# Order of ACT's casts and of the DMA issues of P in a step of hashed attention with a feed-forward network

## The chip, the cores and the metric

One core of a Trainium2 chip. The kernel is one program on that core; its time is the device time in microseconds of one execution. Three runs of the kernel before were timed, and one more execution was profiled. Engines in the text: PE (TensorE, matrix products, with its weight loads PEld), DVE (VectorE), ACT (ScalarE), POOL (GpSimd), SP (SyncE, which issues nearly all DMAs).

## The reference

Attention in which a query sees only the keys that fall in the same hash bucket (six signs of a random projection), and a feed-forward network on the result. q, k and v are 4 x 8 x 768 x 64 (batches, heads, rows, width), the network is 512 to 2048 to 512, all in float32.

```python
q_bits = (np.einsum('bhsd,dk->bhsk', q, proj) > 0)      # k_bits likewise
mask = q_bucket[:, :, :, None] == k_bucket[:, :, None, :]
scores = np.where(mask, scale * np.matmul(q, k.transpose(0, 1, 3, 2)), -1e9)
attn = np.exp(scores - scores.max(-1, keepdims=True))
attn = attn / (attn.sum(-1, keepdims=True) + 1e-9)
x = np.matmul(attn, v).transpose(0, 2, 1, 3).reshape(B * S, H * D)
h = x @ w_in
out = (h * np.clip(h + 3.0, 0.0, 6.0) / 6.0) @ w_out
```

## The kernel before

The attention work is cut into 192 units g: 32 heads (batch by batch), each with six tiles of 128 queries against all 768 keys. The network's work is cut into chunks of 256 tokens, each with 16 slices of the hidden width. Every float32 operand of a product is split into a high part (a cast to the fp32r type) and a low part (the difference), and products are made of high and low parts.

The program has an opening with attention alone, a stretch with network work for batch 0, and from unit GT = 102 on the function `beside_ffn(k)`, one call for each step k, in which a unit of attention and a slice of the network advance together. When the attention is done, the rest of the network runs alone. The order of the instructions on PE, DVE, ACT and POOL is that of the program text; SP's order is set by a planner, which keeps dependences and the orders given by `issue_after(x)`: what is issued inside stands behind x in its queue.

In `beside_ffn(k)` for k of 102 and more a unit g goes through these stages:
- step g - 3, `lead`: the scores on PE (`scores`, L387 and L389).
- step g - 2, `lowest` (the row minimum on DVE, L396), `exponential` (ACT, L408), and `flip` (L426): DVE transposes P in 32 x 32 blocks (L429), and a DMA writes it to a DRAM tile `fd`, one of four.
- step g - 1, `move` (L434): four DMAs, the homes, read `fd` into one of two home tiles (`spare` for even g, `px` for odd g), each 32 rows; this finishes the transpose. A home is free again when unit g - 2 has been split.
- step g + 1, `split_p` (L451) for the two halves c of the keys: ACT casts the high part `ph` (L475); the low part `pl` is made by POOL for c = 1 (L477) and by DVE for c = 0 (L479; it is put in the list `lows`, and `split_lows()` issues it).
- odd step 2u + 3, `values_whole(u)`: the product of v with the units 2u and 2u + 1 together (PE, L513), and in `output` its copy and its DMA.

The network's work of a step is a generator `fill`; `go("A")` to `go("D")` let it advance if its next stage has that letter. A: the gate's cast `gb` (ACT, L689) and its low part (DVE, L690). B: the first product (`gemm1`, L661). C: the second product of the slice before (`gemm2`, L699, L700, L704) and the gate (ACT L683, DVE L684). D: small steps from the list `side` that prepare the next chunk: loads of x, the spread of 1/sum, a transposition of it on PE (`normalise`), the product with x (the list `muls`, issued by `multiply()`, DVE L590), and the splitting of x. `add()` issues the waiting accumulating DMAs from POOL; an entry put in `fresh` waits one call of `add()` longer than one in `adds`.

So in the old order a step of this stretch holds, on ACT: the gate's cast, the exponential of k + 2, the cast of half 1 of unit k - 1, the copy of the output, the gate's first function, the cast of half 0. On DVE: the minimum, the gate's low part, a normalising product if there is one, the transpose, the gate's product, the low part of half 0. In the steps with k % 6 = 2 the minimum comes behind the gate's stage A (`behind`). In SP's queue the write of unit k + 2 stands ahead of the homes of unit k + 1.

Of the kernel before, what the change touches and what calls it, by code (L numbers as in the profile page):

```python
# [28 lines left out]
LA = 3  # L29
# [3 lines left out]
LT = 1  # L33
# [10 lines left out]
def lsh_attention_moe(  # L44
# [10 lines left out]
    nc = tc.nc  # L55
# [3 lines left out]
    KT = S // P  # L59
# [14 lines left out]
    last = None  # L74

    def dma(out: bass.AP, in_: bass.AP):
        nonlocal last
        last = nc.sync.dma_start(out=out, in_=in_)  # L78

    paced = False  # L80
# [147 lines left out]
    NS = NJ * KT  # L228
# [3 lines left out]
    GT = GF + FT  # L232
# [139 lines left out]
    scs, probs, outs = {}, {}, {}  # L372
# [18 lines left out]
    def lowest(g: int):  # L391

        s = scs.pop(g)
        m = sp.tile([P, 1], F32, name=f"m{g}", tag="m", bufs=4)
        pr_ = sp.tile([P, 2, HW], F32, name=f"p{g}", tag="p", bufs=2)
        nc.vector.tensor_scalar(  # L396
            out=pr_[:], in0=s[:, :, :HW], scalar1=CAP, scalar2=None,
            op0=ALU.min, op1=ALU.min, accum_out=m[:],
        )
        probs[g] = pr_, m  # L400
# [20 lines left out]

    written, moved, homes = {}, {}, []

    def flip(g: int):  # L426
        nonlocal written
        x = probs.pop(g)[0][:].rearrange("p c k -> p (c k)")
        nc.vector.transpose(x, x)  # L429
        d = dp.tile([P, S], F32, name=f"fd{g}", tag="fd", bufs=4)  # L430
        dma(out=d[:], in_=x)
        written[g] = d, last

    def move(g: int):  # L434
        if not homes:
            px = sp.tile([P, S], F32, name="px", tag="ga", bufs=1)
            homes.extend([spare[0][:, :S], px[:]])
        to = moved[g] = homes[g % 2]
        d, _ = written.pop(g)
        after = written[g + 1][1] if g + 1 in written else last  # L440
        with tc.issue_after(after.ins):
            for x in range(4):
                r = slice(32 * x, 32 * x + 32)
                dma(
                    out=to[r].rearrange("b (i c) -> b i c", i=4),
                    in_=d[:].rearrange("(i b) (g c) -> g b i c", i=4, g=4)[x],
                )

    lent = []

# [32 lines left out]
    def split_lows():  # L483
        for f in lows:
            f()
        lows.clear()
# [31 lines left out]
    adds, fresh = [], []  # L518
# [10 lines left out]
    def output(un: int):  # L529
        nonlocal vdone  # L530
        i, u = divmod(un, KT // 2)
        b, h = divmod(i, H)
        o = (h % 2) * D
        acc = accs.pop(un)

        if u != 1:
            outs[i] = sp.tile([P, 4 * P if u == 0 else 2 * P], F32, name=f"y{i}_{u}", tag=f"y{u}", bufs=1)
        y = outs[i][:, 2 * P :] if u == 1 else outs[i][:, : 2 * P]

        r = slice(o, o + D)  # L540
        r2 = slice(D - o, 2 * D - o)
        last_head = h == H - 1 and u == (0 if b else 2)
        if last_head:
            nc.scalar.copy(y[r], acc[r2])
            nc.vector.tensor_add(y[r], acc[r], y[r])
        else:
            nc.scalar.copy(y, acc[:])
        if u or last_head:
            single = last_head or h == H - 1 and b
            c = slice(2 * u * P, 2 * (u + 1) * P) if single else slice(0, 4 * P) if u == 1 else slice(4 * P, S)  # L550
            to = xs[b][h * D : (h + 1) * D, c]

            with tc.issue_after(copied.ins):
                dma(out=to, in_=y[r] if single else outs[i][r])
            if not last_head:
                ts = (u,) if single or u else (0, 1)
                (fresh if single and u == 2 else adds).append((i, ts if u != 1 or single else (0, 1), to, y[r2] if single else outs[i][r2]))
        vdone = 2 * un + 2


# [36 lines left out]
    def multiply():  # L597
        for f in muls:
            f()
        muls.clear()  # L600
# [78 lines left out]
    def gate(n: str, fc: int, hg, copy, engine, between=lambda: None):  # L679

        hp, g = hg[:, 0], hg[:, 1]
        r = sp.tile([P, TC], F32, name=f"g{n}_{fc}", tag="g", bufs=1)
        nc.scalar.activation(r[:], hp, AF.Relu, bias=three[:], scale=1.0)  # L683
        nc.vector.scalar_tensor_tensor(out=g, in0=r[:], scalar=6.0, in1=hp, op0=ALU.min, op1=ALU.mult)  # L684
        between()

        def split():
            gh, gl = gate_tiles(f"{n}_{fc}")
            copy(gh, g)  # L689
            engine.tensor_sub(gl, g, gh.bitcast(F32))  # L690
            return gh, gl

        return split
# [31 lines left out]


    xr0, x0 = {}, {}
    side, opening, amid = [], [], []

    def beside():  # L730
        if side:
# [195 lines left out]
    def ffn():  # L927
# [5 lines left out]
        def there(c: int) -> bool:  # L933

            b, t = chunks[c]
            return vdone >= (b + 1) * HK - KT + 2 * (t + 1) and not pending(b, range(H), t)
# [40 lines left out]
        for c, (b, t) in enumerate(chunks):  # L977
            while not there(c):
                if pend is not None:
                    finish()()  # L980
                stage = "B"
                yield
            n = f"{b}_{t}"
            if c not in xr:
                begin(c)
            while side:
                beside()
                stage = "B"
                yield
                if not paced:  # L990
                    yield
            if c not in xhl:
                place(c)
                for cc in range(NCC):
                    split(c, cc)
            ffn_on = True
            copy = nc.scalar.copy
            po = None
            for fc in range(NFC):
                hp = gemm1(n, fc, xhl[c])  # L1000
                stage = "C"
                yield
                end = finish() if pend is not None else lambda: None
                if po is None:
                    po = ps.tile([P, 2, 512], F32, name=f"po{n}", tag="s" if b == B - 1 and t % 2 == 0 else "po", bufs=1)
                parted = paced
                split_g = gate(n, fc, hp, copy, nc.vector, lambda: amid and amid.pop()())
                if not parted:
                    gg = split_g()
                end()  # L1010
                if c + 1 < len(chunks) and c + 1 not in xr and there(c + 1):
                    if fc >= XF[chunks[c + 1][0] == B - 1]:
                        begin(c + 1)
                if parted:
                    stage = "D"
                    yield
                    for _ in range(-(-len(side) // (NFC - fc))):
                        beside()
                if fc + 1 == NFC and c + 1 in xr and c + 1 not in xhl and not side:
                    place(c + 1)  # L1020
                    for cc in range(NCC):
                        split(c + 1, cc)
                elif not parted:
                    beside()
                if parted:
                    stage = "A"
                    yield
                    gg = split_g()
                pend = ((b, t), (fc, [po[:, u] for u in range(2)], *gg))
                stage = "B"  # L1030
                yield
                if not parted:
                    beside()
            del xhl[c]
# [64 lines left out]
    with tc.manual_schedule(engines={ET.PE, ET.DVE, ET.Activation, ET.Pool}):  # L1099
# [9 lines left out]
        def go(part: str):  # L1109
            if stage == part:  # L1110
                next(fill, None)
# [3 lines left out]
        def beside_ffn(k: int):  # L1115
# [9 lines left out]
            for _ in range(2):  # L1125
                u = vnext // 2
# [6 lines left out]
                        through.append(vnext // 2 - 1)  # L1133
                if k < GT:
                    break
            behind = (k - 1 + LA) % KT == 4
            if GT <= k < NS - 2 and not behind:
                lowest(k + 2)
            go("A")
            if GT <= k < NS - 2 and behind:  # L1140
                lowest(k + 2)
            if k < GT:
                for c in range(2):
                    split_p(k, c, False)
# [13 lines left out]
            paced = True  # L1158
            multiply()
            if k + 2 < NS:  # L1160
                flip(k + 2)
            split = GT <= k - LT < NS
            if split:
                split_p(k - LT, 1, False)
            go("B")
            if k == NS + LT:
                homes.clear()
# [2 lines left out]
            hashed = k + LA < NS and (k + LA) % KT == 4 and (k + LA) // KT + 1 < NJ  # L1170
            if hashed:
                hash_qk((k + LA) // KT + 1)
            if split:
                amid.append(lambda: (split_p(k - LT, 0, False), split_lows()))
            go("C")
            while amid:
                amid.pop()()
            split_lows()
            if hashed:
                bits((k + LA) // KT + 1)  # L1180
            if k + LA < NS:
                lead(k + LA)
            if moves:
                moves.pop(0)()
            if GT <= k + 1 < NS:
                move(k + 1)

            place_in_chunk = (k - GT) % NFC
# [6 lines left out]
        for k in range(NS + LT + 2):  # L1195
# [4 lines left out]
            i, t = divmod(k, KT)  # L1200
# [74 lines left out]
        paced = False  # L1275
# [52 lines left out]
```

## Time and profile before

| | |
|---|---|
| median of three runs | 975.12 us (974.37, 975.12, 977.23) |
| the profiled execution | 973.11 us, span 971.3 us |
| granted clock of TensorE | 0.998 |
| PE busy in the span | 948.0 us, 98% |
| DVE, ACT, POOL busy | 723.5, 625.0, 473.6 us |
| first and last `fd` write | 397.1 and 800.8 us, 90 of them |

How to read the rows: a timeline row has the start in us, the duration in us, the engine, the line, the operation, output<-input and a count; in brackets the idle time of the engine ahead of it and what ended it. SPq is SP's queue: the duration is that of the issue, not of the transfer. A row of waits has who waited, for what, the total in us, how often, and the longest. A row of a window has its bounds and length, then for each of PE, PEld, DVE, ACT and POOL the busy time in us with the instructions, then the granted clock, the busy share of the 16 DMA engines and GB/s. A row that starts with a line number and ends with two times has minimum, median and maximum duration in ns, and the first and the last start. A row of DMA issues ends, where the profile knows it, with the median us from issue to landing.

### The profile page before, as it was taken

What the parts mean: (1) busy time and instruction counts of PE and PEld (TensorE: products, weight loads), DVE (VectorE), ACT (ScalarE), POOL (GpSimd) and SP (SyncE); (2) the same over time, 40 slices, a digit from 0 to 9 for tenths busy, and PEclk for the clock granted to TensorE, in tenths of its full rate; (3) what the DMA queues carried; (4) which work ended last, traced back from release to release, by engine and by line L of the source; (5) the groups of instructions that cost most, each with busy time, mean ns of one, the idle gap of its engine ahead of it and who ended that gap; (6) DMA issues with size and microseconds to landing.
All of it is one profiled execution on the core that took longest, in us unless ns stands there. A gap on an engine that the chain in (4) does not pass through costs nothing.

```text
span 971.3 us, 19460 instructions
## 1 busy us (share of the span) xinstructions
PE 948.0 (98%) x6306; PEld 873.6 (90%) x6306; DVE 723.5 (74%) x1470; ACT 625.0 (64%) x1421; POOL 473.6 (49%) x582
## 2 busy tenths in 40 slices
PE   8999999999999999899999999999999999999997
PEld 7999888999989999799899899989899899889896
DVE  7999988888569999877878878878777874342422
ACT  6898875655478988667766666666666664333332
POOL 6777744665537776455555545555545432000000
PEclk9999999999999999999999999999999999999999
DMA  3567579100035554787898788788887772101000
GB/s 117 140 156 188 131 224 377 58 1 1 6 119 119 115 142 112 192 252 233 238 267 234 231 256 241 230 267 236 243 258 233 211 227 71 44 1 44 1 22 22
DMA packets 113613, 152.06 MB, mean 157 GB/s; under 512 B 13876, under 2 KB 82612, under 8 KB 113512
## 3 DMA queue, kind: packets, MB, share of 16 engines
q1 hardware_dynamic: 108472, 144.79, 48.8%
q0 software_dynamic: 5040, 6.03, 5.3%
q8 instruction: 50, 0.82, 0.4%
q14 instruction: 51, 0.42, 0.2%
HBM read 77.34 MB, written 54.00 MB: 135 GB/s over the span
## 4 chain that ended last, share of the span: by engine, by line
PE 79%; DVE 8%; DMA 4%; ACT 4%; issue 3%; POOL 1%; SPq 1%; ACTq 0%; DVEq 0%; POOLq 0%
PE h L661 25%; PE acc L500 6%; PE po L704 6%; PE po L699 6%; PE po L700 6%; PE acc L513 6%; PE pt L418 5%; PE s L389 5%; PE s L387 5%; DMA spare<-fd 2%; DVE p L396 2%; DVE pl L479 2%; ACT ph L475 1%; SPq L78 1%; DVE qq L352 1%
## 5 line engine op out<-in xcount | busy, mean ns | idle before, releaser
L408 ACT ACTIVATE p<-p,m 128x768 f32<-128x768 f32 x192 | 180.2, 939 | 113.4 <-DVE p L396 105.2
L396 DVE TENSOR_SCALAR_CACHE_REDUCE p<-s 128x768 f32<-128x768 f32 x192 | 182.7, 952 | 24.9 <-PE pt L418 12.4
L684 DVE SCALAR_TENSOR_TENSOR h<-g,h 128x256 f32<-128x256 f32 x192 | 81.1, 423 | 102.0 <-ACT g L683 99.0
L683 ACT ACTIVATE g<-h,three 128x256 f32<-128x256 f32 x192 | 91.2, 475 | 94.9 <-PE h L661 94.0
L661 PE MATMUL h<-xh,w 128*128 128x256 f32 x1024 | 146.8, 282 | 0.0
L661 PEld LDWEIGHTS h<-xh,w 128*128 128x128 f32 x1024 | 134.9, 188 | 4.2 <-ACT xh L650 0.6
L429 DVE STREAM_TRANSPOSE p<-p 128x768 f32<-128x768 f32 x90 | 88.1, 979 | 65.2 <-ACT p L408 65.1
L477 POOL TENSOR_TENSOR pl<-spare,ph 128x384 fp32r<-128x384 f32 x45 | 45.8, 1018 | 127.3 <-ACT ph L475 71.4
L479 DVE TENSOR_TENSOR pl<-pt,ph 128x384 fp32r<-128x384 f32 x196 | 100.0, 550 | 4.0 <-ACT ph L475 3.5
L387 PE MATMUL s<-kk,qq 76*128 76x384 f32 x384 | 100.5, 343 | 2.0 <-ACT kk L357 1.5
L389 PE MATMUL s<-kk,qq 128*128 128x384 f32 x384 | 100.4, 343 | 0.0
L700 PE MATMUL po<-w,gb 128*128 128x512 f32 x250 | 98.4, 393 | 0.0
L699 PE MATMUL po<-w,gb 128*128 128x512 f32 x250 | 98.3, 393 | 0.0
L475 ACT CAST ph<-pt 128x384 fp32r<-128x384 f32 x196 | 86.1, 474 | 14.3 <-PE pt L418 13.0
L216 POOL TENSOR_TENSOR w<-wr,w 128x128 fp32r<-128x128 f32 x128 | 71.9, 593 | 45.2 <-ACT w L210 41.9
L418 PE MATMUL pt<-ident,p 128*128 128x128 f32 x612 | 86.2, 275 | 1.9 <-DVE pl L479 1.1
L689 ACT CAST gb<-h 128x256 fp32r<-128x256 f32 x141 | 52.4, 372 | 54.5 <-DVE h L684 26.8
L661 PE MATMUL h<-xl,w 128*128 128x256 f32 x512 | 81.2, 280 | 0.0
L418 PEld LDWEIGHTS pt<-ident,p 128*128 128x128 f32 x612 | 72.5, 141 | 8.9 <-PE pt L418 1.5
L704 PE MATMUL po<-w,gb 128*128 128x512 f32 x250 | 78.6, 395 | 1.5 <-DVE gb L690 1.5
L318 POOL TENSOR_TENSOR kk<-raw,qq 64x192 fp32r<-64x192 f32 (+1 forms) x73 | 65.4, 920 | 25.1 <-ACT qq L304 21.7
L387 PEld LDWEIGHTS s<-kk,qq 76*128 76x128 f32 x384 | 66.6, 190 | 11.7 <-ACT kk L357 2.0
(153 smaller groups left out, 2150.9 us busy)
## 6 DMA issues: line engine op xcount, KB each, us to landing
fd<-p SPq DMA_DIRECT2D x90, 384.0 KB
spare<-fd SPq DMA_DIRECT2D x180, 96.0 KB
px<-fd SPq DMA_DIRECT2D x180, 96.0 KB
kk<-qq SPq DMA_DIRECT2D x62, 192.0 KB
wr<-in_w_in SPq DMA_DIRECT2D x16, 512.0 KB
wr<-in_w_out SPq DMA_DIRECT2D x16, 512.0 KB
raw<-in_qkT SPq DMA_DIRECT2D x19, 384.0 KB
vr<-in_v SPq DMA_DIRECT2D x32, 192.0 KB
```

Source lines behind the costliest of these rows:

```text
L387: nc.tensor.matmul(s[:, c, :HW], lhsT=q1[:KM, us], rhs=half(k1[:KM], c), start=True, stop=False)
L389: nc.tensor.matmul(s[:, c, :HW], lhsT=q2[:, us], rhs=half(k2, c), start=False, stop=True)
L396: nc.vector.tensor_scalar(out=pr_[:], in0=s[:, :, :HW], scalar1=CAP, scalar2=None, op0=ALU.min, op1=ALU.min, accum_out=m[:],)
L408: nc.scalar.activation(pr_[:], pr_[:], AF.Exp, bias=m[:], scale=-1.0, accum_out=sms[b][:, t, h : h + 1])
L418: nc.tensor.transpose(pt[:, x], probs[g][0][:, c, x * P : (x + 1) * P], ident[:])
L475: nc.scalar.copy(hi, pt)
L479: lows.append(lambda: engine.tensor_sub(lo, pt, hi.bitcast(F32)))
L661: nc.tensor.matmul(hp, lhsT=wi[:, wp, wc], rhs=x[cc][xp], start=(k == 0 and cc == 0), stop=(k == 2 and cc == NCC - 1),)
L683: nc.scalar.activation(r[:], hp, AF.Relu, bias=three[:], scale=1.0)
L699: nc.tensor.matmul(po[u], lhsT=gh[:, us], rhs=wo[:, 0], start=(fc == 0), stop=False)
L700: nc.tensor.matmul(po[u], lhsT=gh[:, us], rhs=wo[:, 1], start=False, stop=False)
L704: nc.tensor.matmul(po[u], lhsT=gl[:, us], rhs=wo[:, 0], start=False, stop=(fc == NFC - 1))
```

## The change

In a step of `beside_ffn` from k = 104 on, `multiply()`, both casts of unit k - 1 (half 1, then half 0), the low parts and the homes of unit k + 1 are issued ahead of the gate's stage A, of the exponential and of the transpose. The write of unit k + 2 is ordered behind the last home of unit k + 1 (`brought`). In the steps with k % 6 = 2 the gate's stage A stands between the casts and the low part on DVE. The casts no longer stand behind the exponential and behind the gate's first function. In the step k = 103 the casts stand at the end of the step. The minimum is always the first on DVE. An accumulating DMA that went to `fresh` goes to `adds` in this stretch.

```diff
-    written, moved, homes = {}, {}, []
+    written, moved, homes, brought = {}, {}, [], []
 def flip(g):
         d = dp.tile([P, S], F32, name=f"fd{g}", tag="fd", bufs=4)
-        dma(out=d[:], in_=x)
+        if brought:
+            with tc.issue_after(brought.pop().ins):
+                dma(out=d[:], in_=x)
+        else:
+            dma(out=d[:], in_=x)
 def move(g):
                     in_=d[:].rearrange("(i b) (g c) -> g b i c", i=4, g=4)[x],
                 )
+        brought[:] = [last]
 def output(un):
-                (fresh if single and u == 2 else adds).append(...)
+                (fresh if single and u == 2 and not paced else adds).append(...)
 ffn():
-                split_g = gate(n, fc, hp, copy, nc.vector, lambda: amid and amid.pop()())
+                split_g = gate(n, fc, hp, copy, nc.vector)
 beside_ffn(k):
-            behind = (k - 1 + LA) % KT == 4
-            if GT <= k < NS - 2 and not behind:
+            split = GT <= k - LT < NS
+            if not split or k == GT + 1:
+                go("A")
+            if GT <= k < NS - 2:
                 lowest(k + 2)
-            go("A")
-            if GT <= k < NS - 2 and behind:
-                lowest(k + 2)
+            if split and k - LT > GT:
+                multiply()
+                for c in (1, 0):
+                    split_p(k - LT, c, False)
+                if (k - 1 + LA) % KT == 4:
+                    go("A")
+                split_lows()
+                if k + 1 < NS:
+                    move(k + 1)
+                go("A")
...
             multiply()
             if k + 2 < NS:
                 flip(k + 2)
-            split = GT <= k - LT < NS
-            if split:
-                split_p(k - LT, 1, False)
             go("B")
...
-            if split:
-                amid.append(lambda: (split_p(k - LT, 0, False), split_lows()))
             go("C")
-            while amid:
-                amid.pop()()
-            split_lows()
             if hashed:
                 bits((k + LA) // KT + 1)
+            if split and k - LT == GT:
+                for c in (1, 0):
+                    split_p(GT, c, False)
+                split_lows()
...
-            if GT <= k + 1 < NS:
+            if GT <= k + 1 < NS and not (split and k - LT > GT):
                 move(k + 1)
```

More of the change, by code (lines that the diff above doesn't have):

```diff
@@ L556, in output @@
                 ts = (u,) if single or u else (0, 1)
-                (fresh if single and u == 2 else adds).append((i, ts if u != 1 or single else (0, 1), to, y[r2] if single else outs[i][r2]))
+                (fresh if single and u == 2 and not paced else adds).append((i, ts if u != 1 or single else (0, 1), to, y[r2] if single else outs[i][r2]))
         vdone = 2 * un + 2
@@ L727, in lsh_attention_moe @@
     xr0, x0 = {}, {}
-    side, opening, amid = [], [], []
+    side, opening = [], []
     def beside():
```

## The prediction

> **What bounds the kernel now.** I read the page from the top (busy shares, slices), then the two halves of the run by windows, the waits of the middle stretch, and last the timeline of one pair of steps with the queue of SyncE (SP) beside it.
>
> ```profile
> span 971.3 us, 19460 instructions
> PE 948.0 (98%) x6306; PEld 873.6 (90%) x6306; DVE 723.5 (74%) x1470; ACT 625.0 (64%) x1421; POOL 473.6 (49%) x582
> fd<-p SPq DMA_DIRECT2D x90, 384.0 KB
> ...
> L78 SPq DMA_DIRECT2D fd<-p x90: 320/382/1419, 397.1 to 800.8; - x90
> ...
> 396.00:811.00 415.00, 408.18 (x2646) 375.96 (x2645) 325.81 (x624) 275.07 (x645) 213.12 (x274) 1.00 0.81 239
> 811.00:971.30 160.30, 154.55 (x998) 138.75 (x996) 56.96 (x140) 54.41 (x128) 6.48 (x14) 1.00 0.07 22
> ...
> PE acc L513 <- ACT ph L475: 4.5, 9, 1.5
> PE po L704 <- DVE gb L690: 1.5, 2, 0.8
> ```
>
> Only the stretch 396 to 811 us changes: P goes to DRAM (fd) and back there, 90 times. TensorE (PE) has work in 408.18 of its 415 us, at a granted clock of 1.00. So the most that any better order can give is the idle 6.8 us, and of that the rows name 4.5 us of PE waiting at the value product (L513) for the casts of P, L475, which the change brings forward. The upside is under 1%. The stretch is nearly as full on the DMA side: 0.81 of the engines' time. From 397.1 to 800.8 us the fd writes follow each other every 403.7 / 89 = 4.54 us; that is the length of one step, and every loop of dependences that goes round once per step must stay below it.
>
> The timeline of the queue, where P's round trip stands (the first two rows from a calm place, then three crowded ones), and the landings that rows show:
>
> ```profile
> 801.75 1.76 SPq L78 DMA_DIRECT2D spare<-fd  x4
> 806.02 0.51 ACT L475 CAST ph<-spare 128x384 fp32r<-128x384 f32 x1 [1.38 <-DMA spare<-fd]
> ...
> 569.12 0.53 SPq L78 DMA_DIRECT2D fd<-p  x1
> 569.76 2.33 SPq L78 DMA_DIRECT2D px<-fd  x4
> 572.18 0.40 SPq L78 DMA_DIRECT2D fd<-p  x1
> 573.17 0.81 SPq L78 DMA_DIRECT2D spare<-fd  x2
> ...
> 646.63 0.38 SPq L78 DMA_DIRECT2D fd<-p  x1
> 647.36 1.78 SPq L78 DMA_DIRECT2D spare<-fd  x4
> 651.97 2.21 SPq L78 DMA_DIRECT2D px<-fd  x4
> ...
> SPq L78 <- DMA fd<-p: 3.2, 6, 0.8
> ...
> 0.74 0.38 SPq L78 DMA_DIRECT2D raw<-in_qkT  x1
> 3.95 0.56 DVE L291 CAST qq<-raw 64x768 fp32r<-64x768 f32 x1 [2.16 <-DMA raw<-in_qkT]
> ...
> xs<-y POOLq DMA_DIRECT2D x14, 128.0 KB, 3.7
> xs<-y POOLq DMA_DIRECT2D x16, 64.0 KB, 3.5
> ```
>
> What to see: in the old order the write fd(g) goes out, then the four home loads of the *previous* g, then fd(g+1), and only then the homes of g. The fd of 646.63 is read by the px loads of 651.97, 5.34 us later, with other work of the queue in between. So a write has more than one step to land, and SP waited for such a landing six times only, 3.2 us in all. The fd of 569.12 with its homes at 573.17 is a tight case: 4.05 us, an upper figure for its landing.
>
> **The change part by part.**
>
> *The fd write behind the homes (the main term).* In step k, move(k+1) now comes ahead of flip(k+2), and flip's write is ordered behind the last home load. The homes of k+1 read what fd(k+1) wrote one step before, so SP's queue runs: fd(k+1), wait until it has landed, four home issues, fd(k+2), wait until it has landed, and so on. That is a loop of one step: L = landing of fd + hand-over + four issues + hand-over. It holds nothing that can overlap, since SP issues in order. Its terms:
> - Landing, from the start of the issue: no row gives fd's own. The nearest by size is the first load, also 384 KB, on empty rings: 0.74 to 3.95 = 3.21 us. The POOL queue's rows, smaller but beside the same traffic, have 3.5 and 3.7; the tight case above is at most 4.05. From below: the calm homes of 801.75 end their issues at 803.51 and the cast that waits for them starts at 806.02, so the last 96 KB took 2.5 + 0.45 = about 2.95 us. I take 3.2 by the load of equal size: in the new order the rings are emptier than now when fd goes out, but the homes' last packets are just ahead of it.
> - Four issues: 1.76 and 1.78 where nothing stands between them, 2.21 and 2.33 where the queue is crowded. I take 1.78.
> - Hand-overs: from 569.12 + 0.53 to 569.76 is 0.1 us; twice, 0.2.
>
> L = 3.2 + 1.78 + 0.2 = 5.18 us, against 4.54 available. The chain runs from home(105) to home(191), 86 times: 86 x 0.64 = 55 us. Some of that goes, once, into slack that is there now: ACT's idle time ahead of the exponential (1.13 us, below) and the slack of the gate's low part (0.83, below), together 2 us. Ends: 2.95 + 1.76 + 0.1 = 4.81 gives 23 - 2 = +21; with landings of 3.7 and issues of 2.0 the loop is 5.9 and gives 117 - 2 = +115, about as far as I believe, because a slower step also thins the traffic.
>
> The Trainium skill, "DMA: Bandwidth & Descriptors", section "Anatomy of one DMA — SWDGE (gpsimd) path", fits a DMA's time as a fixed 2.0 us plus bytes over 436 GB/s; for 384 KB that is 2.9 us, an estimate from that page. By it the loop would be 4.9 us and the sum 31 - 2 = 29 us over the time before; no row here times an fd alone. The same page's section "Rules for kernel authors" speaks against the edit: issue a DMA early and wait on its semaphore late, which is what the old order does.
>
> *Queue of SP behind the new wait.* All else that SP issues stands in that queue: loads of q, k, v and x, row moves, stores. In 396 to 811 us it has 160 such DMAs (1.8 a step) of about 0.5 us. I count them at nothing: while SP waits 3 us for a landing five would fit. If half of them are ordered between homes and the next fd instead, L grows by 0.4; that is inside the upper end.
>
> *Casts of P first, the gate's cast behind them.*
>
> ```profile
> ACT p L408 <- DVE p L396: 94.2, 83, 2.9
> ...
> 646.00 0.50 ACT L475 CAST ph<-spare 128x384 fp32r<-128x384 f32 x1
> 646.88 0.38 ACT L689 CAST gb<-h 128x256 fp32r<-128x256 f32 x1 [0.38 <-PE po L704]
> 648.59 0.94 ACT L408 ACTIVATE p<-p,m 128x768 f32<-128x768 f32 x1 [1.34 <-DVE p L396]
> 649.53 0.50 ACT L475 CAST ph<-px 128x384 fp32r<-128x384 f32 x1
> ...
> 646.57 0.72 DVE L479 TENSOR_TENSOR pl<-spare,ph 128x384 fp32r<-128x384 f32 x1
> 647.59 0.96 DVE L396 TENSOR_SCALAR_CACHE_REDUCE p<-s 128x768 f32<-128x768 f32 x1 [0.30 <-PE s L389]
> 648.47 0.42 DVE L690 TENSOR_TENSOR gb<-h,gb 128x256 fp32r<-128x256 f32 x1
> 649.65 0.98 DVE L429 STREAM_TRANSPOSE p<-p 128x768 f32<-128x768 f32 x1 [0.76 <-ACT p L408]
> ...
> 649.72 0.62 PE L704 MATMUL po<-w,gb 128*128 128x512 f32 x2
> ```
>
> ACT stands idle 94.2 / 83 = 1.13 us ahead of the exponential, waiting for the row minimum. Two casts of 0.50 fill that hole, so with the homes in place the move costs nothing and takes away the 4.5 us wait at L513, up to 6.8 with what follows it. With a late home the cover is gone: ACT is in order, and behind the waiting cast stand the gate's cast (then PE's second product), the exponential, and through it the transpose and the next fd. That is how the loop reaches PE.
>
> *The low part and the product ahead of the gate's low part on VectorE.* In the short step the minimum ends at 648.55, the low part takes up to 0.72, and the gate's low part 0.42: it would end at about 649.7, where it ended at 648.89, and L704 takes it at 649.72. So the slack of 0.83 us is just used up. Where a normalising product stands ahead as well (20 of them, 0.41 each), about half fall in short steps and are late by 0.35: 3 to 4 us, at most 12 if all short steps lose 0.3. While the loop binds this hides under it; I take 0. Every sixth step keeps the gate ahead of the low part. The low part no longer follows the gate's product directly; the 0.72 us merely moves within VectorE.
>
> *POOL.* Its low part follows its cast, earlier in the step; POOL is busy 213.12 of 415 us, nothing. Three accumulating DMAs (one for each of the last three batches) go out one turn earlier on the same queue: nothing, they hide behind PE, which never lacks products.
>
> Sum: 973.11 us is the profiled execution (span 971.3); + 55 - 2 = 1026. The median of the three runs is 975.12, 2 us above, inside what I can tell here: 1026 us.
>
> **The rivals.**
> 1. *The loop stays under the step.* If fd lands within 2.6 us, L = 2.6 + 1.76 + 0.1 = 4.5 and does not bind; then PE's wait at L513 goes and the time is 975 - 4.5 to 975 - 6.8: about 969. For it: SP waited for fd only six times, and emptier rings land sooner. Against: no row of a landing is under 2.9, and the old order had a spare position in the queue. It ends on the other side of my forecast. Chance 0.12.
> 2. *The homes arrive, but VectorE's order bites.* The wait at L513 goes and one at L704 comes, by the prices above: -5 + 4 to -5 + 12, so 974 to 982. For it: the 0.83 us used up. Against: it needs case 1's landing first. Chance 0.08, half of it within 0.3%.
> 3. *The loop binds hard.* Other DMAs get between homes and fd, or one of them waits there for an engine: L near 5.9, time 973 + 115 = 1088, give or take 20. Chance 0.15, apart from the main case.
>
> **How the numbers follow.** A loop between 4.8 and 5.7 us, 990 to 1070, has 0.62 and its likeliest value is 1026; harder still 0.15; weak binding (L of 4.6 to 4.8) 0.03. With cases 1 and 2 that is all. Within 0.3% (3 us, about what a measurement of this kernel tells from no change) I put 0.05, faster 0.12, slower 0.83. Range 975 to 1090; it takes in nearly all of case 2 and leaves out case 1 and the far half of case 3. For the likeliest case alone it is 990 to 1070.
>
> **What would show it.** In the new profile the row of SP waiting for fd<-p should grow from 3.2 us to something like one to two us per step; fd issues should stand 5.2 us apart, each right behind four homes, and each group of homes right behind the landing of its own fd; ACT's casts should wait for px and spare; PE's busy share of the stretch should fall to about 87%, with gaps at L513 or the second product; DMA share should fall to about 0.7. I am wrong if the fd issues still come every 4.5 us, or if the SP queue interleaves so that homes never wait for a landing. The casts' part is right if ACT's wait ahead of the exponential for the minimum shrinks by about 1 us, whatever the total does.

## The result and the profile after

The changed kernel is slower: 1028.43 us (median of six runs, 1021.66 to 1032.29) against 975.26 (six runs, 974.37 to 977.23), a ratio of 1.0537, 95% interval 1.0499 to 1.0576. The prediction was 1026. The profiled execution is the shortest of the six, 1021.66 us.

The page after, the rows of the `fd` writes, and the two windows (the attention stretch, which now ends at 860, and the rest):

```profile
span 1019.9 us, 19433 instructions
PE 965.3 (95%) x6306; PEld 874.1 (86%) x6306; DVE 725.5 (71%) x1470; ACT 626.7 (61%) x1421; POOL 472.0 (46%) x582
...
L78 SPq DMA_DIRECT2D fd<-p x90: 320/376/941, 397.0 to 850.4; - x90
...
396.00:860.00 464.00, 425.59 (x2649) 376.47 (x2649) 328.41 (x624) 276.68 (x645) 211.71 (x274) 0.99 0.72 214
860.00:1019.90 159.90, 154.09 (x995) 138.29 (x993) 56.57 (x139) 54.22 (x128) 6.48 (x14) 1.00 0.07 22
```

All the loss lies in the stretch with the `fd` writes: from the first to the last of them 453.4 us where it was 403.7, 49.7 more, and the span grew by 48.6. A step lasts 453.4 / 89 = 5.09 us instead of 4.54. The rest of the run is as before. The granted clock reads 0.99 in the stretch where it was 1.00; one per cent of 464 us is under 5 us, so the clock is not the loss. One thing to read with care: PE is "busy" 425.59 us in the stretch where it was 408.18, with the same instructions. The matmuls that now wait also got longer (in the stretch, L704 has 409 ns each where the same line had 393, and L709 427 where it had 395), so the busy share hides part of the new waiting; the spacing of the writes does not. The rest of the 17 us was not taken apart.

SP's queue in two steps after the change, then the landings of the three writes as the chain of work that ended last gives them (start, us, what):

```profile
601.43 0.37 SPq L78 DMA_DIRECT2D fd<-p  x1
602.13 0.49 SPq L78 DMA_DIRECT2D kk<-qq  x1
602.68 0.59 SPq L78 DMA_DIRECT2D qq<-qq  x1
604.12 1.76 SPq L78 DMA_DIRECT2D spare<-fd  x4
605.98 0.41 SPq L78 DMA_DIRECT2D fd<-p  x1
606.43 0.47 SPq L78 DMA_DIRECT2D kk<-qq  x1
607.71 0.47 SPq L78 DMA_DIRECT2D xs<-y  x1
609.35 1.73 SPq L78 DMA_DIRECT2D px<-fd  x4
611.18 0.38 SPq L78 DMA_DIRECT2D fd<-p  x1
...
601.43 2.61 DMA fd<-p
605.98 3.24 DMA fd<-p
611.18 2.64 DMA fd<-p
```

This is the loop, turn by turn. The write goes out at 601.43, lands 2.61 us later at 604.04; the four homes that read it are issued from 604.12 to 605.88; the next write goes out at 605.98. The turn is 4.55 us, the next one (landing 3.24, homes 1.73) 5.20. In these two turns the other DMAs of the queue stand in the waiting time and cost nothing.

Over the whole stretch it is the same. In the 88 turns of SP's timeline the first home starts 3.11 us after the write on average, the homes take 1.89 us (median 1.75), and the next write follows 0.11 us behind them: 5.11 us together. The landing is not one number, and two of the three above are short ones: the chain holds 51 landings, from 2.46 to 4.76 us, with a mean of 3.15.

Who waits now, in the same stretch:

```profile
SPq L78 <- DMA fd<-p: 110.0, 77, 3.5
...
DVE p L396 <- DMA fd<-p: 86.6, 52, 3.7
ACT p L408 <- DVE p L396: 67.5, 76, 2.3
ACT ph L480 <- DMA px<-fd: 53.7, 38, 3.1
PEld po L709 <- DVE gb L695: 37.2, 50, 2.4
PE po L709 <- DVE gb L695: 16.4, 31, 1.9
PE po L704 <- ACT gb L694: 14.8, 16, 3.5
```

SP's wait for its own writes went from 3.2 us to 110.0. (L480 is the cast of P, L482 POOL's low part of it, L694 and L695 the gate's cast and low part, L704 and L709 the second product, L518 the value product in the new numbering.) The second row is a path that I had not seen: the row minimum writes into one of two P buffers, and the buffer of unit k is free only when its write has landed; a late write therefore holds up the minimum two units later, behind it on DVE the gate's low part, and with that PE at L709. ACT's casts wait for the homes, behind them the gate's cast, and with that PE at L704. The wait of 4.5 us at the value product is gone.

### The profile page after: what moved, and what is told of

Same layout as the page of the kernel before. It is cut to its first block, busy times and chain, and to the rows that moved or that the text cites. A ratio compares the mean times of both kernels' runs of the same rounds, so it can differ in the third digit from the quotient of the medians.

```text
span 1019.9 us, 19433 instructions
## 1 busy us (share of the span) xinstructions
PE 965.3 (95%) x6306; PEld 874.1 (86%) x6306; DVE 725.5 (71%) x1470; ACT 626.7 (61%) x1421; POOL 472.0 (46%) x582
## 4 chain that ended last, share of the span: by engine, by line
PE 59%; DMA 17%; DVE 12%; issue 5%; SPq 4%; POOL 1%; ACT 1%; DVEq 0%; ACTq 0%; POOLq 0%
PE h L666 17%; DMA fd<-p 16%; PE acc L505 6%; PE po L709 5%; PE pt L418 5%; DVE pl L484 4%; PE po L704 4%; PE po L705 4%; SPq L78 4%; PE s L389 4%; PE s L387 4%; PE acc L518 3%; DVE p L396 3%; DVE gb L695 1%; PE z L334 1%
## 5 line engine op out<-in xcount | busy, mean ns | idle before, releaser
L396 DVE TENSOR_SCALAR_CACHE_REDUCE p<-s 128x768 f32<-128x768 f32 x192 | 183.3, 955 | 124.6 <-DMA fd<-p 86.6
L688 ACT ACTIVATE g<-h,three 128x256 f32<-128x256 f32 x192 | 90.7, 473 | 94.2 <-PE h L666 93.4
L666 PE MATMUL h<-xh,w 128*128 128x256 f32 x1024 | 146.4, 282 | 0.0
L666 PEld LDWEIGHTS h<-xh,w 128*128 128x128 f32 x1024 | 135.3, 189 | 3.3
L482 POOL TENSOR_TENSOR pl<-spare,ph 128x384 fp32r<-128x384 f32 x45 | 45.7, 1015 | 155.6 <-ACT ph L480 86.8
L704 PE MATMUL po<-w,gb 128*128 128x512 f32 x250 | 101.3, 405 | 15.1 <-ACT gb L694 14.8
L709 PE MATMUL po<-w,gb 128*128 128x512 f32 x250 | 84.2, 418 | 17.0 <-DVE gb L695 16.4
L705 PE MATMUL po<-w,gb 128*128 128x512 f32 x250 | 98.3, 393 | 0.0
L480 ACT CAST ph<-pt 128x384 fp32r<-128x384 f32 x196 | 86.2, 473 | 14.5 <-PE pt L418 13.2
L709 PEld LDWEIGHTS po<-w,gb 128*128 128x128 f32 x250 | 43.2, 189 | 44.0 <-DVE gb L695 37.2
L666 PE MATMUL h<-xl,w 128*128 128x256 f32 x512 | 80.7, 279 | 0.0
```

The costliest lines, as they stand in the source:

```text
L396: nc.vector.tensor_scalar(out=pr_[:], in0=s[:, :, :HW], scalar1=CAP, scalar2=None, op0=ALU.min, op1=ALU.min, accum_out=m[:],)
L666: nc.tensor.matmul(hp, lhsT=wi[:, wp, wc], rhs=x[cc][xp], start=(k == 0 and cc == 0), stop=(k == 2 and cc == NCC - 1),)
L704: nc.tensor.matmul(po[u], lhsT=gh[:, us], rhs=wo[:, 0], start=(fc == 0), stop=False)
L705: nc.tensor.matmul(po[u], lhsT=gh[:, us], rhs=wo[:, 1], start=False, stop=False)
L709: nc.tensor.matmul(po[u], lhsT=gl[:, us], rhs=wo[:, 0], start=False, stop=(fc == NFC - 1))
```

## The experiments

Every kernel was compared with the kernel before on the same chip. Medians, ratios to before with their 95% intervals:

| kernel | us | ratio |
|---|---|---|
| casts_first_old_dma_order | 994.40 | 1.0193 (1.0167 to 1.0218) |
| old_compute_write_behind_homes | 1043.56 | 1.0695 (1.0671 to 1.0719) |
| two_homes_ahead_of_write | 1000.58 | 1.0257 (1.0232 to 1.0283) |
| six_home_issues | 1098.52 | 1.1265 (1.1222 to 1.1307) |
| gate_cast_ahead_again | 974.12 | 0.9989 (0.9976 to 1.0002) |
| write_behind_homes_gate_ahead | 1031.43 | 1.0574 (1.0552 to 1.0596) |
| two_ahead_gate_ahead | 996.04 | 1.0199 (1.0166 to 1.0231) |
| three_ahead_gate_ahead | 1008.88 | 1.0344 (1.0301 to 1.0387) |
| write_from_acts_queue | 992.62 | 1.0184 (1.0161 to 1.0206) |
| write_from_acts_queue_gate_ahead | 981.54 | 1.0070 (1.0056 to 1.0084) |
| both_casts_behind_exponential | 989.61 | 1.0160 (1.0137 to 1.0184) |
| both_casts_and_low_part_ahead | 984.28 | 1.0099 (1.0086 to 1.0113) |

**The DMA order undone, the casts kept.**

```diff
 (after)
                 split_lows()
-                if k + 1 < NS:
-                    move(k + 1)
                 go("A")
...
             if k + 2 < NS:
+                brought.clear()
                 flip(k + 2)
+            if split and k - LT > GT and k + 1 < NS:
+                move(k + 1)
```

> The changed kernel with the DMA order of before put back: the write of unit k + 2 is issued ahead of the homes of unit k + 1. The casts of P stay first in ACT's step, the low part stays ahead of the gate's low part. Theory A (the loop write, landing, four home issues, next write, once per step in SP's queue): the loop is gone, SP's wait for fd falls from 110 us to under 10, the fd writes follow each other at about 4.5 us again, and the time is 968 to 978 (the 4.5 us wait at the value product gone, up to 10 us given back at the gate's low part). Theory B (the casts at the head of ACT's step wait for homes and hold up the gate behind them, whatever SP's order): the time stays at 1010 to 1030.

994.40 us: between the two. The first four rows are its waits, the last its writes:

```profile
SPq L78 <- DMA fd<-p: 1.6, 4, 0.5
...
ACT ph L480 <- DMA px<-fd: 58.8, 38, 3.5
ACT ph L480 <- PE acc L518: 50.4, 32, 3.2
...
PE po L704 <- ACT gb L694: 14.9, 18, 3.3
...
L78 SPq DMA_DIRECT2D fd<-p x90: 319/343/2027, 397.6 to 822.7; - x90
```

SP's wait for fd was down to 1.6 us, so the loop was gone, and 34 us of the loss with it. But 19 us stayed: the casts at the head of ACT's step find the px homes not yet landed, and the gate's cast behind them is late for PE. The casts wait nearly as long for PE's value product (third row), but that is not what PE pays for: in 17 of the 18 waits at L704 the cast ahead of the gate's cast had waited for px.

**The DMA order alone, in the compute order of before.**

```diff
 (before)
 def flip(g):    # from unit GT + 4 on
-        dma(out=d[:], in_=x)
+        writes.append(write)        # write(): the same dma, issue_after the last home
...
                 move(k + 1)
+            while writes:
+                writes.pop(0)()
```

> The kernel before with the DMA order of the change alone: the write of unit k + 2 is issued behind the homes of unit k + 1; the order of ACT, DVE, PE and POOL is that of before. Theory A: the loop of 5.0 us per step is there, so the time is 1010 to 1040, and SP waits for fd about 100 us. Theory B: the casts stand late in ACT's step, so homes are there when they are wanted; 973 to 985.

1043.56 us. Theory A's side, and 4 us beyond its upper end. Its wait for fd and its writes:

```profile
SPq L78 <- DMA fd<-p: 95.4, 62, 4.1
...
L78 SPq DMA_DIRECT2D fd<-p x90: 320/430/1519, 397.1 to 874.4; - x90
```

So the DMA order by itself makes the loss, without any cast moved. It costs 15 us more than the whole change. In its attention stretch SP also waits 41.1 us for the gate's cast and low part, where it waited 7.3 us for the low part in the changed kernel; whether that is the extra was not tried.

**Two issues more in the loop.**

```diff
 (after, move)
             for x in range(4):
-                r = slice(32 * x, 32 * x + 32)
-                dma(...)                              # 32 rows
+                for y in range(0, 32, 16 if x < 2 else 32):
+                    n = 16 if x < 2 else 32
+                    r = slice(32 * x + y, 32 * x + y + n)
+                    dma(...)                          # n rows
```

> The changed kernel with two of the four home loads cut into two of 16 rows each: the same bytes in six issues of SP in place of four, all ahead of the next write. Theory A: the loop grows by two issues of 0.3 to 0.44 us, to 5.6 to 5.9 us; 86 turns give 52 to 75 us more, so 1080 to 1105. Theory B: homes land up to 0.9 us later in a step; in a step of 5.1 us with waits of about 0.1 us for them that costs as much at most if nothing gives, but part of it hides in the idle time ahead of the exponential: 1030 to 1060.

1098.52 us, 70 more than the changed kernel. Its queue and its writes:

```profile
601.62 0.38 SPq L78 DMA_DIRECT2D fd<-p  x1
602.11 0.49 SPq L78 DMA_DIRECT2D kk<-qq  x1
602.65 0.58 SPq L78 DMA_DIRECT2D qq<-qq  x1
603.29 0.59 SPq L78 DMA_DIRECT2D kk<-qq  x1
604.32 2.85 SPq L78 DMA_DIRECT2D spare<-fd  x6
607.26 0.38 SPq L78 DMA_DIRECT2D fd<-p  x1
...
L78 SPq DMA_DIRECT2D fd<-p x90: 319/376/1517, 397.8 to 929.8; - x90
```

A step lasts 532.0 / 89 = 5.98 us, 0.89 more, for two more issues of the same bytes. On average over the turns six issues take 2.82 us where four took 1.89, 0.93 more (medians 2.67 and 1.75), and the time from the write to the first home stays at 3.11. A term of the loop was changed and the step followed it. Theory B's range ended at 1060.

**Two of four homes ahead of the write.**

```diff
 (after)
-                    move(k + 1)
+                    move(k + 1, range(2) if k + 2 < NS else range(4))
...
                 flip(k + 2)
+                if split and k - LT > GT:
+                    move(k + 1, range(2, 4))      # the other two, behind the write
+                    brought.clear()
```

> The changed kernel, but only two of the four home issues stand ahead of the write of the next unit, the other two behind it. Theory A: the loop is landing 2.93 + hand-overs 0.2 + two issues 0.87 = 4.0 us, less than a step of 4.54, so it doesn't bind: 968 to 985, with SP's wait for fd well under half of 110 us. Theory B: the casts wait for the last homes, which are issued no earlier than in the changed kernel; 1010 to 1030.

1000.58 us: 28 less than with four, and 6 more than with none. It missed Theory A's range, and SP's wait for fd, 67.9 us, is not well under half of 110. The range left out the 19 us of the gate's cast, which the first kernel of this group showed, but that is not the whole reason: with the gate's cast ahead (two_ahead_gate_ahead, below) the time is still 11 us above the range.

**The gate's cast ahead again, old DMA order.** This kernel is aimed at those 19 us.

```diff
 (casts_first_old_dma_order)
             if split and k - LT > GT:
+                go("A")
                 multiply()
                 for c in (1, 0):
```

> As casts_first_old_dma_order, but the gate's stage A (its cast on ACT and its low part on DVE) stands ahead of the casts of P again; the casts still stand ahead of the exponential. That kernel kept 19 us of loss with PE waiting 14.9 us at L704 for the gate's cast, which stood behind casts that waited for px. Theory C (only the gate's cast behind a late home costs): the wait at L704 goes and the time is 968 to 978. Theory D (a second loop, two steps long: casts that wait for homes, then exponential, transpose, write, the homes behind that write, about 8.5 to 9 us against 9.1 in two steps): the gate's place doesn't matter to the loop, the wait moves from L704 to the value product or to the scores, and the time stays at 985 to 1000.

974.12 us (12 runs), no difference from before that can be told. Theory C. The casts still wait for px (first row), but nothing that PE needs soon stands behind them:

```profile
ACT ph L480 <- DMA px<-fd: 40.4, 33, 2.5
...
PE po L709 <- DVE gb L695: 2.5, 2, 2.2
PE h L666 <- DVE xl L656: 1.5, 2, 0.8
PE po L704 <- ACT gb L694: 1.4, 3, 0.5
PE acc L518 <- POOL pl L482: 0.9, 3, 0.4
```

It also shows what the casts' move is worth: the 4.5 us wait at the value product is down to 0.9, and waits at L709, L704 and the first product (L666) came in its place.

**The same with the homes ahead of the write: the loop alone.** The edit is the same `go("A")`, in the changed kernel.

> The changed kernel with its DMA order (homes ahead of the next write), but the gate's stage A ahead of the casts of P, as in gate_cast_ahead_again, which ran at the time of before (974 us). It prices the loop in SP's queue alone. Theory A: a step lasts one turn of the loop, 5.0 us, so 1010 to 1030, with SP waiting about 100 us for fd and no wait of PE for the gate's cast at L704 worth naming. If the gate's place were most of the loss, 974 to 990.

1031.43 us, 1 us above Theory A's range:

```profile
SPq L78 <- DMA fd<-p: 118.7, 71, 4.4
...
DVE p L396 <- DMA fd<-p: 108.3, 59, 4.3
PE po L709 <- DVE gb L695: 34.2, 32, 2.7
PE po L704 <- ACT gb L694: 0.9, 2, 0.5
```

So with the gate out of the way the DMA order costs 1031 - 974 = 57 us, the whole loss of the change; and the gate's place, 20 us without the loop (994 against 974), costs nothing with it (1028 against 1031). The two prices don't add: while the loop sets the step, the late gate's cast lies beside it. Here PE meets the loop through the P buffers and L709 instead of L704. What that path costs by itself was not tried; a third P buffer would be the test.

**Two and three homes ahead, gate ahead.** The edits above combined.

> As write_behind_homes_gate_ahead (1031 us), but only two of the four home issues stand ahead of the next write. Turn of the loop: 2.93 + 0.2 + 0.87 = 4.0 us, below the 4.54 of a step. Theory A: it doesn't bind, 972 to 985.

> As two_ahead_gate_ahead with three home issues ahead of the next write. Turn of the loop: 2.93 + 0.2 + 1.31 = 4.44 us, just under a step of 4.54 with single turns above it: 978 to 1000, between the kernels with two and with four.

996.04 and 1008.88 us, both above their ranges, by 11 and 9 us. With none, two, three and four issues ahead of the write: 974, 996, 1009, 1031. The order is as the loop wants it, but the threshold that I expected is not there: with two ahead the turn should be 4.0 us and not bind, and yet it costs 22 us.

```profile
SPq L78 <- DMA fd<-p: 68.3, 48, 2.5
...
L78 SPq DMA_DIRECT2D fd<-p x90: 319/376/1532, 397.5 to 827.9; - x90
```

SP still waits for fd in 48 of the steps. The rows are those with two ahead, and SP's timeline of that run shows which term of the sum was too small. In its 86 turns the first home of the next unit starts 3.79 us after the write on average, where the sum had a landing of 2.93 and a hand-over of 0.1; the two homes ahead take 0.90, and the next write follows 0.20 us behind them (median 0.10, so it seldom waits for its transpose). That is 4.88 us, above 4.54, so the loop still binds. With three ahead the terms are 3.60, 1.37 and 0.10, 5.07 us. Why the next homes start later after the write than in the changed kernel (3.11 us) was not tried; the homes that now go out right behind the write are one candidate. Steps also vary in length, and a step that the loop has lengthened isn't made up, since PE has next to no idle time.

**The write from ACT's queue.**

```diff
 (after, flip)
-            with tc.issue_after(brought.pop().ins):
-                dma(out=d[:], in_=x)
+            writes.append(lambda: nc.scalar.dma_start(out=d[:], in_=x))
...
             go("C")
+            while writes:
+                writes.pop(0)()
```

> The changed kernel with the write of P issued from ACT's own queue, behind the gate's first function of the step; the casts stay first and the homes stay early in SP's queue, and no home stands ahead of a write any more. Theory A plus D: both loops are cut, since a write waits for no home and a home only for its own write: 966 to 980 (about 0.05 to 0.5 us of ACT's time per issue, 90 issues). If instead the casts at the head of ACT's step are themselves the loss (homes land too late for them however the queue is ordered), L704 keeps its wait and the time is 990 or more.

> As write_from_acts_queue, with the gate's stage A ahead of the casts. Neither the loop (the write is in another queue) nor the gate's cast behind a late home is left: 966 to 975. If it stays at 985 or more, the write from ACT's queue has a price of its own (ACT waiting for the transpose, or the late write).

992.62 us, and 981.54 with the gate ahead. The first lies in the range of the second branch, although the wait at L704 fell from 14.8 to 7.7 us. In the second neither loop nor gate's cast is left, but it is 7 us slower than before: PE waited 8.9 us at the value product for POOL's low part of P (ten times). That time lies above the range and below the 985 from which the write from ACT's queue was to have a price of its own. The write now leaves behind the gate's first function and SP waits 53.3 us for it, so the homes come later; and each of the 88 issues takes 0.33 us of ACT's queue. Which of these is the cause was not tried apart.

**Only the two casts together, behind the exponential.**

```diff
 (before)
             if split:
-                split_p(k - LT, 1, False)
+                for c in (1, 0):
+                    split_p(k - LT, c, False)
+                split_lows()        # in the second kernel only
...
-                amid.append(lambda: (split_p(k - LT, 0, False), split_lows()))
+                amid.append(split_lows)        # in the first kernel only
```

> The kernel before with one change on ACT: the cast of half 0 of P stands directly behind that of half 1, behind the exponential and ahead of the output's copy and the gate's first function. DMA order and all else as before. The wait of 4.5 us at the value product came from the cast of half 0 behind the gate's first function, which waits for the first product. If that is right and theory D too (casts behind the exponential are not in a loop with the write): 967 to 973, the wait gone. If casts anywhere earlier find late homes: 975 to 985.

> As both_casts_behind_exponential, with the low part of half 0 on VectorE directly behind the transpose, ahead of the gate's product. There the wait at the value product had only moved from the cast to the low part (5.6 us, 17 times, for L479 behind the gate's product). If the low part's place was the whole cause, the time is 965 to 973; if the gate's first function behind two casts costs by itself, 980 to 990.

989.61 and 984.28 us. The first is above both of its ranges, and the homes were not late there: its casts waited for px once, 0.8 us. The wait moved from the cast to the low part, which stands behind the gate's product on DVE:

```profile
642.07 0.91 ACT L475 CAST ph<-px 128x384 fp32r<-128x384 f32 x2
643.80 0.48 ACT L683 ACTIVATE g<-h,three 128x256 f32<-128x256 f32 x1
644.32 0.43 DVE L684 SCALAR_TENSOR_TENSOR h<-g,h 128x256 f32<-128x256 f32 x1 [1.14 <-ACT g L683]
644.66 0.55 DVE L479 TENSOR_TENSOR pl<-px,ph 128x384 fp32r<-128x384 f32 x1
645.26 0.63 PE L513 MATMUL acc<-pl,vv 128*128 128x256 f32 x3 [0.93 <-DVE pl L479]
```

Moving the low part as well gave back 5 us of 15, so its place was not the whole cause. The time lies in the range that was given for a price of the gate's first function behind two casts, but the trace does not single that out: there PE's weight loads waited 8.7 us for POOL's low part (24 times). What the other 10 us are was not settled. None of the kernels beat the one before.

## Why the prediction was right

**The loop.** It was the step that decided, and it held: write, landing, four issues, next write, once per step. The step became 5.09 us against 5.18 by the sum, and 86 x (5.09 - 4.54) = 47 us against 55 - 2. The landing was 3.2 in the sum; the 51 landings in the chain after have a mean of 3.15. That the mean came out so close is in part luck: 3.2 was taken from another transfer, and single landings lie between 2.46 and 4.76. The fit of the Trainium skill's page "DMA: Bandwidth & Descriptors" ("Anatomy of one DMA — SWDGE (gpsimd) path") had given 2.9 us, an estimate for another queue; the measured mean is 0.25 us longer, and the 29 us worked out from the fit are short of the measured 53. The four issues were 1.78 in the sum and measured 1.89 on average (median 1.75), the hand-overs 0.1 as taken. That the other DMAs cost nothing held in the rows shown: they fill the wait. Undoing this part gave back 34 us, and 57 with the gate's cast out of the way; doing it alone cost 68; two issues more cost 70, inside their range of 52 to 75. Only the shortened loops, with two and three homes ahead, did not follow their sums: their landing term was too small.

**The casts.** The step "with the homes in place the move costs nothing" had a premise that fails: without the loop the homes of px are not in place either, 38 waits of 58.8 us in all, and the gate's cast behind them costs PE 20 us. The prediction had this cascade (a late home, the gate's cast, PE's second product), but only as the way in which the loop reaches PE. The rival "the loop stays under the step, about 969" was therefore wrong in its time as well: without the loop the kernel takes 994. So was the ACT row: the wait ahead of the exponential shrank only from 1.13 to 67.5 / 76 = 0.89 us each, since the minimum itself came later. Without the loop it does shrink as forecast: 13.4 us in 15 waits in gate_cast_ahead_again, where it was 94.2 us in 83.

**The upside.** At most 6.8 us, 4.5 of it named, was read as a bound. It is not a strict one, since busy time can hold waiting, as the profile after shows. With the casts first and the gate ahead of them the named wait went, and the time did not move (0.9989, 0.9976 to 1.0002): other waits took its place.

**The path from the write to PE** was told as one chain through ACT's casts. There is a second, through the two P buffers and the row minimum (86.6 us of DVE's waiting). It changed no number, because both hang on the same loop.

**What it would show.** SP's wait of one to two us per step: 110.0 us over 87 steps is 1.3. DMA share about 0.7: 0.72. PE busy about 87%: it reads 425.59 / 464 = 92%, because part of the waiting is counted in; the old busy time over the new length is 88%.

## What to carry to other kernels

When two DMAs of an in-order queue are exchanged, follow the semaphores round: a read placed ahead of the next write, where the read waits for the last write, makes a loop of landing plus issues, and its turn has to be shorter than the step. The landing in that sum is the one of the new order, which can differ from the old: from the write to the first home it took 3.11 us with all four loads ahead of the write and 3.79 with two on either side. An instruction that may wait for a transfer should not stand ahead of one that the busiest engine needs soon, even if its own engine has idle time there. Prices of two such faults are taken apart one at a time: here 57 and 20 us alone, and 53 together.

## What was not expected of the hardware

A write of 384 KB issued directly behind four loads lands in 2.46 to 4.76 us (51 landings, mean 3.15), and cutting the same loads into more DMAs makes SP's issue longer by about 0.46 us for each (medians 1.75 us for four, 2.67 for six). PE's recorded busy time can grow without work: 948.0 us before, 965.3 after, for the same 6306 matmuls.
